# Attention stage of a three-layer kernel: wider matmul streams, other accumulator banks, a shorter step pipeline

## The chip, the cores and the metric

The kernel runs on one core of a Trainium2 chip. The metric is device time in microseconds (us). The kernel before was timed three times: 2105.6, 2106.95 and 2112.1, median 2106.95. A fourth execution was profiled; all rows below come from that one.

The core has a matmul engine (PE, with weight loads shown apart as PEld), a vector engine (DVE), an activation engine (ACT), a general engine (POOL) and a queue that issues transfers (SP). Each takes its instructions in program order. PE writes only to PSUM, which has eight banks of 128 x 512 float32 values.

## The reference

Three layers follow each other: a linear attention with exponential features, a gated layer, and a layer of eight experts. Only the first is touched.

```
q, k, v: (4 batches, 8 heads, 576 tokens, 64); omega: (128, 64)
def phi(x):
    proj = einsum('bhsd,md->bhsm', x, omega)
    h = proj - sum(x*x, axis=-1, keepdims=True)/2
    return exp(h - max(h, axis=-1, keepdims=True)) / sqrt(128)
q_p, k_p = phi(q*scale), phi(k*scale)
kv  = einsum('bhsm,bhsd->bhmd', k_p, v);  z = sum(k_p, axis=2)
num = einsum('bhsm,bhmd->bhsd', q_p, kv)
den = einsum('bhsm,bhm->bhs', q_p, z)[..., None] + 1e-06
x = (num/den) as a matrix (2304 tokens, 512);  out = experts(gated(x))
```

## The kernel before

The attention works through 36 chunks, k and q chunks in turn. A normal chunk holds 512 tokens of two heads (4 blocks of 128 tokens for each head); the remaining 64 tokens of each batch are gathered in two k and two q tail chunks (numbers 0 and 17, 18 and 35). Each chunk passes through a chain of small stages, and the chunks are pipelined by hand: the loop at L639 counts steps, and the table `ORDER` (L63) lists pairs of a stage and an offset. In each step the stages run down the table, stage with offset n on chunk step - n. So the table fixes the order of instructions on every engine.

The stages of one chunk, with the names of tiles in the profile (`two`, `bank` in PSUM; `at` and `turned` in SBUF):

- `s0`, `s0r`, `s0n` (L470, L475, L480): squares on POOL, their sum on DVE, its scaling on ACT.
- `s2p` (L497): projection on PE into one of two double banks `two`; 8 matmuls, two at a time in the two row halves of the array. Offset 1.
- `s2m` (L505): row maximum on DVE; `s2b`, `s2c` (L511, L515): the bias on POOL; `s2x` (L521): 8 exponentials on ACT. Offset 2.
- `s3`: of a k chunk the sums k'v and z, 5 matmuls for each of the two heads (L536, L537), moving 66 columns (64 of v, one of ones, one spare); of a q chunk 8 transposes (L541). Offset 4. The two halves are placed apart in a step: `s30` before the projection, `s31` after it.
- `s3a`: ACT copies what `s3` left in PSUM (L550 for k, L554 for q). Offset 5.
- `s4` (L570; L568 for a tail): numerators and denominators of a q chunk, 4 matmuls of 66 columns for each head; `s4d`, `s4r`, `s4n` (L582, L587, L592) divide on DVE. Offset 6.
- `s5` (L602): 4 transposes of the result; `s5a` (L613) on ACT and `s5b` (L618) on DVE split it in a high and a low part. Offset 7.
- `pump`: twice a step, one piece of background work that converts the weights of the next layer on ACT, DVE and POOL (L192 to L210).
- `warm` (L501): products of an identity matrix with itself, 24 in the first steps, whose results nobody reads.

float32 matmuls show as two records each; the transposes as one. `RINGS` (L67) assigns PSUM banks to uses: turned features `tr3` banks 0 and 3, turned output `tr5` bank 0, k-v sums bank 3, numerators banks 1 and 2. A new use of a bank waits until its last reader is done.

From step 38 on (`step >= NCH + 2`) the gated layer is interleaved with the last steps of the attention; its first matmul is L693. From there on PE has work without a break.

Of the kernel before, what the change touches and what calls it, by code (L numbers as in the profile page):

```python
# [13 lines left out]
AF = mybir.ActivationFunctionType  # L14
ALU = mybir.AluOpType
# [5 lines left out]
P = 128  # L21
B, H, S, D = 4, 8, 576, 64
M = 128
# [18 lines left out]
ZW = D + 2  # L42
# [8 lines left out]
class Kernel:  # L51
    def __init__(self, tc, x, v, vt, omega, wg, wv, wo, w2g, w1, w2, out):
# [7 lines left out]

    ORDER = [("s3a0", 5), ("s3a1", 5), ("s40", 6), ("s41", 6), ("s30", 4), ("s5", 7), ("s2p", 1), ("s31", 4), ("warm", 1),  # L63
             ("s2m", 2), ("s2b", 2), ("s2c", 2), ("s0r", 0), ("s0", -1), ("s5a", 7), ("s5b", 7), ("s2x0", 2), ("s2x1", 2),
             ("s0n", 0), ("s4d0", 6), ("s4d1", 6), ("s4r", 6), ("s4n0", 6), ("s4n1", 6), ("pump", 3), ("pump", 4)]
    WARM = (2, 10, 6, 4, 2)
    RINGS = dict(tr3=(0, 3), tr5=(0,), kv=(3,), nu=(1, 2), a=(0, 1, 2, 3), b=(4, 5, 6, 7))  # L67

    DRAIN = dict(RINGS, tr3=(4, 5), tr5=(6, 4, 5), nu=(7, 6))

# [287 lines left out]
    def run(self):  # L358
        tc, nc = self.tc, self.nc
        with ExitStack() as ctx:  # L360
# [9 lines left out]
            self.twos = [psum.tile([P, 1024], F32, tag=f"b{i}", name=f"two{i}") for i in range(2)]  # L370
            self.turns, self.rings, self.nquad = {}, self.RINGS, 0
            ident = self.cst.tile([P, P], F32, name="ident")
# [23 lines left out]
    def attention(self, m1):  # L396
        tc, nc = self.tc, self.nc
        if True:
# [6 lines left out]
            t5 = af.tile([P, 10, 2, ZW], F32, tag="t5", name="at5")  # L405
# [3 lines left out]
            def turn(name, n):  # L409
                rot[name] = (rot.get(name, -1) + 1) % n  # L410
                return rot[name]
# [6 lines left out]
            vz = [t4[:, i] for i in range(NVZ)]  # L418
# [7 lines left out]
            chunks = [("k", 0, None, None)]  # L426
# [8 lines left out]
            NCH = len(chunks)  # L435
            st = [dict() for _ in chunks]
            kvz = {}
# [3 lines left out]
            def load(i):  # L441
                side, bp, hp, j = chunks[i]
                c = st[i]
                n = 8 if hp is None else 2 * hp + j
                k = turn("x", 3)
                xt = c["xt"] = xts[turn("xt", 4)]
                c["x"] = t0[:, k].rearrange("p (a d) -> p a d", d=D)
                for w, t in ((1, xt), (0, t0[:, k])):
                    nc.sync.dma_start(t, self.x["qk".index(side), w, bp, n])
                c["idx"] = (lambda a, h: 2 * a + h) if hp is None else (lambda a, h: 4 * h + a)  # L450

            def loadv(i):
                side, bp, hp, j = chunks[i]
                c = st[i]
                if side == "q":
                    return
                if hp is None:
                    c["vz"] = vzts[2 * bp:2 * bp + 2]
                    for j in range(2):
                        nc.sync.dma_start(c["vz"][j].rearrange("p a d -> p (a d)"), self.vt[bp, j])  # L460
                else:
                    z = c["vz"] = vz[nvz[0] % NVZ]
                    nvz[0] += 1
                    nc.sync.dma_start(z.rearrange("p a d -> p (a d)"), self.v[bp, 2 * hp + j])

            def s0(i):
                c = st[i]
                x = c["x"]
                xx = c["xx"] = t0[:, 3].rearrange("p (a d) -> p a d", d=D)
                nc.gpsimd.tensor_tensor(xx, x, x, op=ALU.mult)  # L470
# [28 lines left out]
            def warm(i):  # L499
                for _ in range(self.WARM[i] if i < len(self.WARM) else 0):  # L500
                    nc.tensor.matmul(self.banks[1][:, 0:P], ident, ident, start=True, stop=True)  # L501
# [15 lines left out]
            def s2x(i, u):  # L517
                c = st[i]
                e, bi, pr = c["e"], c["bi"], c["pr"]
                for n in range(4 * u, 4 * u + 4):  # L520
                    nc.scalar.activation(e[:, n, :], pr[:, n % 2, n // 2, :], AF.Exp, bias=bi[:, n:n + 1])  # L521

            def s3(i, h):
                side, bp, hp, j = chunks[i]
                c = st[i]
                e = c["e"]
                if side == "k":
                    if hp is None:
                        ek_tail[bp] = (e, c["vz"])
                        return  # L530
                    et, vt = ek_tail[bp]
                    if h == 0:
                        c["kv"] = self.bank("kv", 2, ZW)
                    kv = c["kv"]
                    for a in range(4):
                        nc.tensor.matmul(kv[:, h, :], e[:, c["idx"](a, h), :], c["vz"][:, c["idx"](a, h), :], start=(a == 0), stop=False)  # L536
                    nc.tensor.matmul(kv[:, h, :], et[:, 2 * hp + h, :], vt[j][:, 2 * hp + h, :], start=False, stop=True)  # L537
                else:
                    tr = self.bank("tr3", 4, P)
                    for a in range(4):  # L540
                        nc.tensor.transpose(tr[:, a, :], e[:, c["idx"](a, h), :], ident)  # L541
                    c["tr3", h] = tr

            def s3a(i, h):
                side, bp, hp, j = chunks[i]
                c = st[i]
                if side == "k":
                    if h == 1 and hp is not None:
                        z = t5[:, turn("z", 10)]
                        nc.scalar.activation(z, c["kv"], AF.Copy, scale=1.0 / M)  # L550
                        kvz[bp, hp, j] = z
                else:
                    t = t2[:, turn("et", 4)].rearrange("p (a t) -> p a t", t=P)
                    nc.scalar.copy(t, c["tr3", h])  # L554
                    c["et", h] = t

            def s4(i, h):
                side, bp, hp, j = chunks[i]
                if side == "k":
                    return  # L560
                c = st[i]
                nu = self.bank("nu", 4, ZW)
                for a in range(4):
                    t = c["et", h][:, a, :]
                    if hp is None:
                        for b in range(2):
                            r = slice(b * TL, (b + 1) * TL)
                            nc.tensor.matmul(nu[r, a, :], t[:, r], kvz[bp, a, b][:, h, :], start=True, stop=True)  # L568
                    else:
                        nc.tensor.matmul(nu[:, a, :], t, kvz[bp, hp, j][:, h, :], start=True, stop=True)  # L570
                c["nu", h] = nu

            def s4d(i, h):
                side, bp, hp, j = chunks[i]
# [44 lines left out]
                st[i] = None  # L619

            pump = lambda i: self.attn_pump()
            fns = dict(s0=s0, s0r=s0r, s0n=s0n, s2p=s2p, s2m=s2m, s2b=s2b, s2c=s2c, s4r=s4r, s5=s5, s5a=s5a, s5b=s5b, warm=warm, pump=pump)
            halves = dict(s2x=s2x, s3=s3, s3a=s3a, s4=s4, s4d=s4d, s4n=s4n)

            def stage(n):
                if n in fns:
                    return fns[n]
                g, h = halves[n[:-1]], int(n[-1])
                return lambda i: g(i, h)

            order = [(stage(n), k) for n, k in self.ORDER]
            load(0)
# [3 lines left out]
                nc.tensor.matmul(self.banks[1][:, 0:P], ident, ident, start=True, stop=True)  # L636
            nc.vector.tensor_scalar(om2, om, SCALE, None, op0=ALU.mult)
            s0(0)
            for step in range(NCH + 7):  # L639
                if step == NCH + 2:  # L640
                    self.rings = self.DRAIN
                    self.upper.close()
                    psum = self.upper.enter_context(tc.tile_pool(name="upper", bufs=1, space=PSUM))
                    self.banks += [psum.tile([P, 512], F32, tag=f"b{i}", name=f"bank{i}") for i in range(4, 8)]
                if step + 2 < NCH:
                    load(step + 2)
                if 0 < step <= NCH:
                    loadv(step - 1)
                for fn, n in order:
                    i = step - n  # L650
                    if 0 <= i < NCH:
                        fn(i)
                self.attn_hook(step)
                if step >= NCH + 2:
                    next(m1)

    def attn_hook(self, step):
        if step == 2:
            self.make_tasks()
            self.load_tasks(self.ahead)  # L660
            self.enqueue(6)
# [862 lines left out]
```

## Time and profile before

| what | us |
|---|---|
| median of three runs | 2106.95 |
| the profiled execution | 2111.08 |
| its span in the trace | 2109.3 |
| first matmul of the gated layer (L693) in the trace | 181.51 |
| busy in the span: PE, DVE, ACT, POOL | 2064.3, 1358.7, 810.1, 1003.3 |

The page shows PE busy for 98% of the span, and at 9 tenths or more in nearly all of its 40 slices; the slices below that are in the first 10%. The granted clock of PE is 0.7 in the first slice of the page and 0.9 or more in the others; a slice is 53 us long, so shorter stretches need a closer view. A record of a matmul lasts longer than the distance to the next one, because successive matmuls overlap: what a stream of them costs is read from the starts of successive rows.

### The profile page before, as it was taken

To read this page: it belongs to the slowest core of one execution; us is meant where nothing else is said; L and a number is where in the kernel's file an instruction comes from. 1 tells how busy PE (TensorE), PEld (TensorE's weight loads), DVE (VectorE), ACT (ScalarE), POOL (GpSimd) and SP (SyncE) were. 2 spreads that over 40 slices of the span, in tenths; PEclk is the share of its full clock that TensorE was granted. 3 is DMA by queue.
4 is the path that set the end of the run, shared out by engine and by line. 5 is a ranking of instruction groups with operands and counts; after the bars stand their busy time and mean duration, and the time that the engine had idled before them with its cause. 6 is when DMAs were issued, how large, how long until landed. Compare 5 with 4: busy or idle time off the path is not lost.

```text
span 2109.3 us, 32863 instructions
## 1 busy us (share of the span) xinstructions
PE 2064.3 (98%) x12044; PEld 1992.7 (94%) x12044; DVE 1358.7 (64%) x2175; ACT 810.1 (38%) x1840; POOL 1003.3 (48%) x1014
## 2 busy tenths in 40 slices
PE   8989999999999999999999999999999999999998
PEld 7878999999998889989888999999999999999998
DVE  4764778788755744444445666666688666666666
ACT  5765433333344444334333423233233433323322
POOL 3442657656533455455552544434454544443443
PEclk7999999999999999999999999999999999999999
DMA  5552555555424666666768788877887878877784
GB/s 197 172 161 67 184 167 182 186 165 178 150 86 155 219 219 242 256 224 256 261 226 307 247 262 260 261 260 247 303 262 259 281 259 262 261 259 255 249 273 153
DMA packets 238129, 467.78 MB, mean 222 GB/s; under 512 B 20272, under 2 KB 110096, under 8 KB 233872
## 3 DMA queue, kind: packets, MB, share of 16 engines
q1 hardware_dynamic: 237968, 465.68, 65.6%
q8 instruction: 95, 1.56, 0.3%
q14 instruction: 66, 0.54, 0.1%
HBM read 340.25 MB, written 125.35 MB: 221 GB/s over the span
## 4 chain that ended last, share of the span: by engine, by line
PE 91%; DVE 4%; ACT 2%; issue 1%; POOL 1%; DMA 0%; SPq 0%; DVEq 0%; POOLq 0%; ACTq 0%
PE bank L1049 13%; PE bank L1295 7%; PE bank L1296 7%; PE bank L1297 7%; PE pair L1386 7%; PE pair L1387 7%; PE pair L1388 7%; PE bank L694 5%; PE bank L695 5%; PE bank L693 5%; PE bank L990 4%; PE bank L992 4%; PE bank L991 3%; PE bank L725 2%; PE bank L727 2%; PE bank L726 2%
## 5 line engine op out<-in xcount | busy, mean ns | idle before, releaser
L1398 DVE TENSOR_TENSOR sums<-pair,sums 128x768 f32<-128x768 f32 x209 | 198.8, 951 | 44.3 <-PE pair L1388 44.3
L1295 PE MATMUL bank<-xh,ar 128*128 128x384 f32 x564 | 188.7, 335 | 2.4 <-ACT mt L1328 2.0
L1296 PE MATMUL bank<-xl,ar 128*128 128x384 f32 x564 | 188.4, 334 | 0.0
L1297 PE MATMUL bank<-xh,ar 128*128 128x384 f32 x564 | 188.4, 334 | 0.0
L1065 DVE SCALAR_TENSOR_TENSOR ac<-bank,mt,ac 128x512 f32<-128x512 f32 x84 | 63.1, 751 | 132.5 <-PE bank L1049 128.8
L1386 PE MATMUL pair<-xh,ar 128*128 128x384 f32 x344 | 115.0, 334 | 0.2 <-DVE sums L1398 0.2
L1387 PE MATMUL pair<-xl,ar 128*128 128x384 f32 x344 | 114.9, 334 | 0.0
L1388 PE MATMUL pair<-xh,ar 128*128 128x384 f32 x344 | 114.9, 334 | 0.0
L1295 PEld LDWEIGHTS bank<-xh,ar 128*128 128x128 f32 x564 | 105.8, 188 | 3.4 <-ACT mt L1328 2.7
L1296 PEld LDWEIGHTS bank<-xl,ar 128*128 128x128 f32 x564 | 105.9, 188 | 0.0
L1297 PEld LDWEIGHTS bank<-xh,ar 128*128 128x128 f32 x564 | 105.9, 188 | 0.0
L707 ACT CAST ar<-mt 128x384 fp32r<-128x384 f32 x72 | 37.0, 514 | 170.6 <-DVE mt L704 170.6
L693 PE MATMUL bank<-xh,ar 128*128 128x384 f32 x288 | 96.6, 336 | 0.0
L695 PE MATMUL bank<-xh,ar 128*128 128x384 f32 x288 | 96.2, 334 | 0.0
L695 PE MATMUL bank<-xh,ar1b 128*128 128x384 f32 x288 | 96.2, 334 | 0.0
L694 PE MATMUL bank<-xl,ar 128*128 128x384 f32 x288 | 96.2, 334 | 0.0
L693 PE MATMUL bank<-xh,ar1b 128*128 128x384 f32 x288 | 96.2, 334 | 0.0
L694 PE MATMUL bank<-xl,ar1b 128*128 128x384 f32 x288 | 96.2, 334 | 0.0
L990 PE MATMUL bank<-xh,ar 128*128 128x384 f32 x264 | 89.5, 339 | 3.3 <-DVE st L1024 2.5
L992 PE MATMUL bank<-xh,ar 128*128 128x384 f32 x264 | 88.8, 336 | 0.6 <-DVE ar L262 0.5
L991 PE MATMUL bank<-xl,ar 128*128 128x384 f32 x264 | 88.3, 335 | 0.0
L1049 PE MATMUL bank<-ar,xh 128*128 128x512 f32 x324 | 85.4, 397 | 0.0
(379 smaller groups left out, 6700.8 us busy)
## 6 DMA issues: line engine op xcount, KB each, us to landing
ar<-w2forms SPq DMA_DIRECT2D x144, 512.0 KB, 4.5
ar<-w1forms SPq DMA_DIRECT2D x141, 512.0 KB, 4.9
ar1b<-w1forms SPq DMA_DIRECT2D x62, 512.0 KB, 4.9
ar1b<-w2forms SPq DMA_DIRECT2D x61, 512.0 KB, 4.5
w2forms<-ar SPq DMA_DIRECT2D x224, 128.0 KB, 4.1
w1forms<-ar SPq DMA_DIRECT2D x22, 1280.0 KB, 7.6
sumsraw<-in_w_dram SPq DMA_DIRECT2D x32, 512.0 KB, 4.3
w2forms<-sumsraw SPq DMA_DIRECT2D x128, 128.0 KB, 2.7
```

Source lines behind the costliest of these rows:

```text
L693: nc.tensor.matmul(t, hi[:, c, fs], self.xh[:, c, cs], start=(c == 0), stop=False)
L694: nc.tensor.matmul(t, hi[:, c, fs], self.xl[:, c, cs], start=False, stop=False)
L695: nc.tensor.matmul(t, lo[:, c, fs], self.xh[:, c, cs], start=False, stop=(c == KC - 1))
L990: nc.tensor.matmul(g, ah[:, c, :], bh[:, c, :], start=(first and c == 0), stop=False, skip_group_check=not first)
L1049: nc.tensor.matmul(y, a, w[:, fi % 2, ds], start=(first and x == 0 and k == 0 and fi == fis[0]), stop=(last and x == 1 and fi == fis[-1]))
L1295: nc.tensor.matmul(g, w[:, 0, d], bh[:, d, :], start=bool(first and d == 0), stop=False, skip_group_check=not first)
L1296: nc.tensor.matmul(g, w[:, 0, d], bl[:, d, :], start=False, stop=False, skip_group_check=not first)
L1297: nc.tensor.matmul(g, w[:, 1, d], bh[:, d, :], start=False, stop=(d == 1), skip_group_check=not first)
L1386: nc.tensor.matmul(y, w[:, k, 0, ds], h, start=(k == 0), stop=False)
L1387: nc.tensor.matmul(y, w[:, k, 0, ds], l, start=False, stop=False)
L1388: nc.tensor.matmul(y, w[:, k, 1, ds], h, start=False, stop=(k == 1))
L1398: v.tensor_tensor(a[n], pair, a[n], op=ALU.add)
```

## The change

A k-v matmul and a numerator matmul now stream 128 columns where they streamed 66: `wide` takes a window of 128 neighbouring columns that holds the 66 wanted ones, at its start for the first head and at its end for the second. What is wanted stands in columns 0 to 65 or 62 to 127 of the result, and only that is read. The k-v sums use bank 2 (with the second head's numerators) instead of bank 3, the turned output bank 1 (with the first head's numerators) instead of bank 0. The copy of the k-v sums goes from ACT to a new stage `s3k` on DVE, in the step of the sums. `s3` has offset 3 instead of 4, and `s3a`, `s4`, `s5` follow at 4, 5, 6; both halves of `s3` now stand before the projection, `s5` before `s3`. v is loaded one step earlier, the background work begins one step later, there are 30 warming products instead of 24, and one step less.

```
-    ORDER = [("s3a0", 5), ("s3a1", 5), ("s40", 6), ("s41", 6), ("s30", 4), ("s5", 7), ("s2p", 1), ("s31", 4), ...
+    ORDER = [("s3a0", 4), ("s3a1", 4), ("s40", 5), ("s41", 5), ("s5", 6), ("s30", 3), ("s31", 3), ("s2p", 1), ...
-    WARM = (2, 10, 6, 4, 2)
-    RINGS = dict(tr3=(0, 3), tr5=(0,), kv=(3,), nu=(1, 2), a=(0, 1, 2, 3), b=(4, 5, 6, 7))
+    WARM = (2, 10, 8, 6, 4)
+    RINGS = dict(tr3=(0, 3), tr5=(1,), kv=(2,), nu=(1, 2), a=(0, 1, 2, 3), b=(4, 5, 6, 7))
+            OFF = (0, P - ZW)
+            def wide(t, n, h):
+                o = n * ZW - OFF[h]
+                return t.rearrange("p a d -> p (a d)")[:, o:o + P]
...
-                        c["kv"] = self.bank("kv", 2, ZW)
-                    kv = c["kv"]
+                        c["kv"] = self.bank("kv", 380)
+                    kv = c["kv"][:, h * P:(h + 1) * P]
...
-                        nc.tensor.matmul(kv[:, h, :], e[:, c["idx"](a, h), :], c["vz"][:, c["idx"](a, h), :], start=(a == 0), stop=False)
+                        nc.tensor.matmul(kv, e[:, n, :], wide(c["vz"], n, h), start=(a == 0), stop=False)
...
-                        nc.scalar.activation(z, c["kv"], AF.Copy, scale=1.0 / M)
...
+            def s3k(i):
+                    kv = st[i]["kv"].rearrange("p (h c) -> p h c", h=2)[:, :, 0:ZW]
+                    nc.vector.tensor_scalar(z, kv, 1.0 / M, None, op0=ALU.mult)
...
-                nu = self.bank("nu", 4, ZW)
+                nu = self.bank("nu", 4, P)
+                own = nu[:, :, OFF[h]:OFF[h] + ZW]
...
-                        nc.tensor.matmul(nu[:, a, :], t, kvz[bp, hp, j][:, h, :], start=True, stop=True)
+                        nc.tensor.matmul(nu[:, a, :], t, wide(kvz[bp, hp, j], h, h), start=True, stop=True)
...
-            for step in range(NCH + 7):
+            for step in range(NCH + 6):
-                if 0 < step <= NCH:
-                    loadv(step - 1)
+                if step < NCH:
+                    loadv(step)
...
-        if step == 2:
+        if step == 3:
             self.make_tasks()
```

Two steps on PE (one that sums a k chunk, one that turns a q chunk) in the kernel before; L602 is `s5`, L497 `s2p`, L536 and L537 the k-v sums, L570 the numerators, L541 the turned features:

```order
L602 MATMUL bank_69<-ident,at_97 128x128 x4
L497 MATMUL two_76<-om_100,turned 128x128 x8
L536 MATMUL bank_72<-at_98,at_95 128x66 x4
L537 MATMUL bank_72<-at_98,at_97 128x66
L570 MATMUL bank_70<-at_99,at_96 128x66 x4
L570 MATMUL bank_71<-at_99,at_96 128x66 x4
L541 MATMUL bank_69<-ident,at_95 128x128 x4
L497 MATMUL two_77<-om_100,turned 128x128 x8
L541 MATMUL bank_72<-ident,at_95 128x128 x4
L536 MATMUL bank_72<-at_98,turned 128x66 x4
L537 MATMUL bank_72<-at_98,at_97 128x66
```

The same in the changed kernel, where L613 is `s5`, L543 and L545 the k-v sums, L581 the numerators and L549 the turned features:

```order
L613 MATMUL bank_70<-ident,at_97 128x128 x4
L543 MATMUL bank_71<-at_98,at_95 128x128 x4
L545 MATMUL bank_71<-at_98,at_97 128x128
L543 MATMUL bank_71<-at_98,at_95 128x128 x4
L545 MATMUL bank_71<-at_98,at_97 128x128
L497 MATMUL two_77<-om_100,turned 128x128 x8
L581 MATMUL bank_70<-at_99,at_96 128x128 x4
L581 MATMUL bank_71<-at_99,at_96 128x128 x4
L549 MATMUL bank_69<-ident,at_95 128x128 x4
L549 MATMUL bank_72<-ident,at_95 128x128 x4
L497 MATMUL two_76<-om_100,turned 128x128 x8
```

The projection now ends each step, the k-v sums no longer follow a transpose into their own bank (bank_72 is the fourth, bank_71 the third), and the number of instructions is the same.

Two steps on DVE before, with `s2m` (L505), `s0r` (L475), the division (L582 to L592), `s5b` (L618) and a piece of background work (L203):

```order
L505 TENSOR_REDUCE mx_510<-two_77 128x8
L475 TENSOR_REDUCE ssq_583<-at_94 128x8
L618 TENSOR_TENSOR xl<-bank_69,xh 128x512
L203 TENSOR_SCALAR m1raw_0_1_188<-cv 128x512
L505 TENSOR_REDUCE mx_564<-two_76 128x8
L475 TENSOR_REDUCE ssq_635<-at_94 128x8
L582 TENSOR_SCALAR den_648<-bank_70 128x4
L582 TENSOR_SCALAR den_648<-bank_71 128x4
L587 RECIPROCAL rec_649<-den_648 128x8
L592 TENSOR_TENSOR at_97<-bank_70,rec_649 128x4x64
L592 TENSOR_TENSOR at_97<-bank_71,rec_649 128x4x64
```

And in the changed kernel, where L629 is `s5b` and L565 is `s3k`:

```order
L505 TENSOR_REDUCE mx_486<-two_76 128x8
L475 TENSOR_REDUCE ssq_556<-at_94 128x8
L629 TENSOR_TENSOR xl<-bank_70,xh 128x512
L565 TENSOR_SCALAR at_99<-bank_71 128x132
L196 TENSOR_SCALAR cv<-cv 128x512
L198 TENSOR_SCALAR cv<-cv 128x512
L505 TENSOR_REDUCE mx_542<-two_77 128x8
L475 TENSOR_REDUCE ssq_608<-at_94 128x8
L593 TENSOR_SCALAR den_621<-bank_70 128x4
L593 TENSOR_SCALAR den_621<-bank_71 128x4
L598 RECIPROCAL rec_622<-den_621 128x8
L603 TENSOR_TENSOR at_97<-bank_70,rec_622 128x4x64
```

One instruction has come in, L565 behind `s5b`; what was queued behind `s5b`, the background work and the next step's maximum, is now queued behind L565.

## Rows read from the trace of the kernel before

**Rows 1.** Windows of the trace: busy time (count) by engine, granted clock, DMA share

```profile
28.00:55.50 27.50, 26.83 (x150) 24.36 (x149) 11.06 (x22) 11.67 (x41) 5.47 (x10) 0.50 0.29 97
57.62:93.15 35.53, 32.12 (x322) 28.85 (x322) 25.19 (x46) 26.35 (x91) 18.25 (x31) 1.00 0.55 178
181.51:2109.30 1927.79, 1904.91 (x10619) 1849.31 (x10617) 1249.53 (x1979) 694.51 (x1441) 930.69 (x883) 1.00 0.67 227
```

**Rows 2.** Timeline of PE, two steps: start, length, line, records, [idle before, releaser]

```profile
66.38 0.60 PE L602 MATMUL bank<-ident,at 128*128 128x128 f32 x4
66.91 1.16 PE L497 MATMUL two<-om,turned 64*128 64x128 f32 x16
68.00 1.11 PE L536 MATMUL bank<-at,at 128*128 128x66 f32 x8
...
69.17 1.95 PE L570 MATMUL bank<-at,at 128*128 128x66 f32 x16
70.96 0.61 PE L541 MATMUL bank<-ident,at 128*128 128x128 f32 x4
71.49 1.16 PE L497 MATMUL two<-om,turned 64*128 64x128 f32 x16
72.59 0.66 PE L541 MATMUL bank<-ident,at 128*128 128x128 f32 x4
73.97 1.11 PE L536 MATMUL bank<-at,turned 128*128 128x66 f32 x8 [0.73 <-ACT at L554]
...
75.14 0.60 PE L602 MATMUL bank<-ident,at 128*128 128x128 f32 x4
```

**Rows 3.** Waits of PE from 0 to 200 us: total us, times, longest

```profile
PE bank L536 <- ACT at L554: 15.2, 15, 2.4
```

**Rows 4.** Timeline of PE in the first 33 us

```profile
8.89 2.50 PE L501 MATMUL bank<-ident 128*128 128x128 f32 x20
13.01 1.16 PE L497 MATMUL two<-om,turned 64*128 64x128 f32 x16 [1.63 <-ACT at L521]
14.10 2.60 PE L501 MATMUL bank<-ident 128*128 128x128 f32 x12
...
32.73 3.62 PE L570 MATMUL bank<-at,at 128*128 128x66 f32 x16
```

**Rows 5.** Timeline of PE, two steps at the low clock, first and last row

```profile
43.13 1.06 PE L602 MATMUL bank<-ident,at 128*128 128x128 f32 x4
...
57.62 0.61 PE L602 MATMUL bank<-ident,at 128*128 128x128 f32 x4
```

**Rows 6.** Windows of 5 us: columns as in Rows 1

```profile
15.00:20.00 5.00, 5.00 (x39) 4.65 (x39) 3.36 (x6) 3.04 (x12) 1.64 (x4) 0.71 0.82 269
110.00:115.00 5.00, 5.00 (x39) 4.44 (x40) 1.97 (x3) 3.24 (x12) 0.00 (x0) 0.66 0.23 80
145.00:150.00 5.00, 3.52 (x27) 3.15 (x28) 2.47 (x4) 2.62 (x7) 2.67 (x4) 0.76 0.35 105
```

**Rows 7.** Groups by line, 57.62 to 93.15 us: count | busy us, mean ns | idle before

```profile
L505 DVE TENSOR_REDUCE mx<-two 128x8 f32<-128x1024 f32 x8 | 9.7, 1218 | 0.7 <-PE two L497 0.7
L475 DVE TENSOR_REDUCE ssq<-at 128x8 f32<-128x512 f32 x8 | 5.4, 676 | 0.0
L592 DVE TENSOR_TENSOR at<-bank,rec 128x256 f32<-128x256 f32 x8 | 3.0, 420 | 0.1
L618 DVE TENSOR_TENSOR xl<-bank,xh 128x512 fp32r<-128x512 f32 x4 | 2.8, 692 | 7.0 <-ACT xh L613 7.0
L582 DVE TENSOR_SCALAR den<-bank 128x4 f32<-128x4 f32 x8 | 1.3, 160 | 2.6 <-PE bank L570 2.6
L554 ACT COPY at<-bank 128x512 f32<-128x512 f32 x8 | 4.8, 626 | 0.4 <-PE bank L541 0.4
L511 POOL TENSOR_TENSOR hm<-mx,nsq 128x8 f32<-128x8 f32 x8 | 1.6, 201 | 14.8 <-DVE mx L505 14.6
```

**Rows 8.** Timeline of ACT, the exponentials of one chunk

```profile
58.74 2.18 ACT L521 ACTIVATE at<-two,bi 128x128 f32<-128x128 f32 x8
```

**Rows 9.** Timeline of PE: waits before two stages, first matmul of the gated layer

```profile
146.53 1.11 PE L536 MATMUL bank<-at,at 128*128 128x66 f32 x8 [1.48 <-ACT at L554]
...
181.51 0.42 PE L693 MATMUL bank<-xh,ar 128*128 128x384 f32 x1
181.77 0.34 PE L694 MATMUL bank<-xl,ar 128*128 128x384 f32 x1
181.95 0.33 PE L695 MATMUL bank<-xh,ar 128*128 128x384 f32 x1
```

More of the change, by code (lines that the diff above doesn't have):

```diff
@@ L58, in __init__ @@
         self.bg = deque()
-    ORDER = [("s3a0", 5), ("s3a1", 5), ("s40", 6), ("s41", 6), ("s30", 4), ("s5", 7), ("s2p", 1), ("s31", 4), ("warm", 1),
-             ("s2m", 2), ("s2b", 2), ("s2c", 2), ("s0r", 0), ("s0", -1), ("s5a", 7), ("s5b", 7), ("s2x0", 2), ("s2x1", 2),
-             ("s0n", 0), ("s4d0", 6), ("s4d1", 6), ("s4r", 6), ("s4n0", 6), ("s4n1", 6), ("pump", 3), ("pump", 4)]
-    WARM = (2, 10, 6, 4, 2)
-    RINGS = dict(tr3=(0, 3), tr5=(0,), kv=(3,), nu=(1, 2), a=(0, 1, 2, 3), b=(4, 5, 6, 7))
+    ORDER = [("s3a0", 4), ("s3a1", 4), ("s40", 5), ("s41", 5), ("s5", 6), ("s30", 3), ("s31", 3), ("s2p", 1), ("warm", 1),
+             ("s2m", 2), ("s2b", 2), ("s2c", 2), ("s0r", 0), ("s0", -1), ("s5a", 6), ("s2x0", 2), ("s2x1", 2), ("s0n", 0),
+             ("s4d0", 5), ("s4d1", 5), ("s4r", 5), ("s4n0", 5), ("s4n1", 5), ("s5b", 6), ("s3k", 3), ("pump", 3), ("pump", 4)]
+    WARM = (2, 10, 8, 6, 4)
+    RINGS = dict(tr3=(0, 3), tr5=(1,), kv=(2,), nu=(1, 2), a=(0, 1, 2, 3), b=(4, 5, 6, 7))
     DRAIN = dict(RINGS, tr3=(4, 5), tr5=(6, 4, 5), nu=(7, 6))
@@ L532, in s3 @@
                     if h == 0:
-                        c["kv"] = self.bank("kv", 2, ZW)
-                    kv = c["kv"]
+                        c["kv"] = self.bank("kv", 380)
+                    kv = c["kv"][:, h * P:(h + 1) * P]
                     for a in range(4):
-                        nc.tensor.matmul(kv[:, h, :], e[:, c["idx"](a, h), :], c["vz"][:, c["idx"](a, h), :], start=(a == 0), stop=False)
-                    nc.tensor.matmul(kv[:, h, :], et[:, 2 * hp + h, :], vt[j][:, 2 * hp + h, :], start=False, stop=True)
+                        n = c["idx"](a, h)
+                        nc.tensor.matmul(kv, e[:, n, :], wide(c["vz"], n, h), start=(a == 0), stop=False)
+                    n = 2 * hp + h
+                    nc.tensor.matmul(kv, et[:, n, :], wide(vt[j], n, h), start=False, stop=True)
                 else:
@@ L546, in s3a @@
                 c = st[i]
-                if side == "k":
-                    if h == 1 and hp is not None:
-                        z = t5[:, turn("z", 10)]
-                        nc.scalar.activation(z, c["kv"], AF.Copy, scale=1.0 / M)
-                        kvz[bp, hp, j] = z
-                else:
+                if side == "q":
                     t = t2[:, turn("et", 4)].rearrange("p (a t) -> p a t", t=P)
@@ L555, in s3a @@
                     c["et", h] = t
+            def s3k(i):
+                side, bp, hp, j = chunks[i]
+                if side == "k" and hp is not None:
+                    z = kvz[bp, hp, j] = t5[:, turn("z", 10)]
+                    kv = st[i]["kv"].rearrange("p (h c) -> p h c", h=2)[:, :, 0:ZW]
+                    nc.vector.tensor_scalar(z, kv, 1.0 / M, None, op0=ALU.mult)
             def s4(i, h):
@@ L567, in s4 @@
                             r = slice(b * TL, (b + 1) * TL)
-                            nc.tensor.matmul(nu[r, a, :], t[:, r], kvz[bp, a, b][:, h, :], start=True, stop=True)
+                            nc.tensor.matmul(own[r, a, :], t[:, r], kvz[bp, a, b][:, h, :], start=True, stop=True)
                     else:
-                        nc.tensor.matmul(nu[:, a, :], t, kvz[bp, hp, j][:, h, :], start=True, stop=True)
-                c["nu", h] = nu
+                        nc.tensor.matmul(nu[:, a, :], t, wide(kvz[bp, hp, j], h, h), start=True, stop=True)
+                c["nu", h] = own
             def s4d(i, h):
@@ L621, in attention @@
             pump = lambda i: self.attn_pump()
-            fns = dict(s0=s0, s0r=s0r, s0n=s0n, s2p=s2p, s2m=s2m, s2b=s2b, s2c=s2c, s4r=s4r, s5=s5, s5a=s5a, s5b=s5b, warm=warm, pump=pump)
+            fns = dict(s0=s0, s0r=s0r, s0n=s0n, s2p=s2p, s2m=s2m, s2b=s2b, s2c=s2c, s4r=s4r, s5=s5, s5a=s5a, s5b=s5b, s3k=s3k, warm=warm, pump=pump)
             halves = dict(s2x=s2x, s3=s3, s3a=s3a, s4=s4, s4d=s4d, s4n=s4n)
```

## The prediction

> **What bounds the kernel now.** I began with the page: PE is busy for 98% of the span, and what is missing lies at the start. Windows of the trace [rows 1] part it: from 181.5 us to the end PE is busy for 98.8% at the full granted clock (1.00, that is 2.4 GHz), so what comes before shifts the rest rigidly, and the change is worth what it takes off those first 181.5 us. There the reader is to see two different losses. From 28 to 55.5 us the clock is at 0.50 (1.2 GHz), though PE is busy for 26.8 of 27.5 us; between 57.6 and 93.2 us it is at 1.00, and PE is busy for 32.1 of 35.5 us: it waits. The timeline of two steps [rows 2] shows where: after the second half of the transposes it stands 0.73 us for ACT's copy at L554, since the k-v sums go to the bank that these transposes have just filled. The list of waits [rows 3] counts 15 of these, 15.2 us in all.
>
> From the same starts I read what each stage takes on PE at the full clock [rows 2]: output transposes 0.53 (66.38 to 66.91), projection 1.09, a half of the sums 1.17 (68.00 to 69.17), the numerators 1.79, a half of the turning 0.53.
>
> **128 columns.** 16 k chunks with 10 sums and 16 q chunks with 8 numerators, two records each: 576 records get 62 columns more. What this costs is read from the identity products, which already stream 128: 20 records in 2.50 us [rows 4], 0.125 each, against 16 records of 66 columns in 1.95 [rows 2], 0.122 each. So between 0 and 576 x 0.003 = 1.7 us; I take 0, since the first distance after a projection is in the longer figure. The other bound is a column's price in a long stream: 384 columns in 0.18 us [rows 9], 0.47 ns each, 62 of them 29 ns, 576 times 16.8 us. It can't be below nothing, as no instruction goes.
> The Trainium skill speaks against the edit here ("TensorE: Matmul & The Clock Gate", Back-to-back issue gap): the distance of single matmuls grows by N/2.4 ns, which would make 62 columns cost an estimated 25.8 ns, 14.9 us in all. The two rows just compared do not show it at 66 and 128 columns. The same page (LDWEIGHTS) gives P/1.2 for a weight load, 107 ns for 128 columns, whatever is streamed after it.
>
> **The clock.** Two steps took 14.49 us at the low level [rows 5] and 8.76 at the full one [rows 2]. The low stretch began after waits and went on for 27 us with 66-column matmuls in every step. In the window at 15 us, where identity products and projections run, the clock dropped as well (0.71) and was back soon [rows 4, 6]; the drops at 110 and 145 us were as short (0.66, 0.76). The streams of the changed kernel are like those of the window at 15 us, so I take the short form (0.66 in a window of 5 us is 3.4 us at the half level, 1.7 us lost). The other end is a stretch like that of before, 27 us, whose price is half of it, 13.6 us.
>
> **A step put together.** A step that sums now holds output transposes, both halves of the sums and the projection: 0.53 + 2.34 + 1.09 = 3.96. A step that turns holds numerators, both halves, projection: 1.79 + 1.06 + 1.09 = 3.94. Two steps 7.90 in place of 8.76, if nothing waits. What could:
> - The sums' bank is now the second of the numerators. Its reader is the division on DVE, in the step before; the output transposes, which now come first in the step, need that division anyway. DVE starts a turning step with the maximum 1.22 and the sum 0.68, then 2 x 0.16, a reciprocal (as L582, 0.16) and 2 x 0.42 [rows 7]: done at 3.2 to 3.3 of 3.94 us. Slack 0.6. In the kernel before, half of the sums stood ahead of these transposes.
> - The numerators' first bank must be free of the output (L618 on DVE, done by about 2.6 in the step before) and the second of the sums' copy. That copy moves to DVE; no row has its form. Bounds: 0.16 (L582, 16 elements at most) and 0.42 (L592, 256 elements); by size I take 0.3. DVE's load per two steps is 25.19 / 4 = 6.3 [rows 1], then 6.6 of 7.9; ACT loses as much. The copy waits for the sums (2.87 into the step, when DVE is through 1.22 + 0.68 + 0.69 = 2.6) and ends near 3.4. Behind it on DVE stand the background work and the next maximum, for which ACT waits; half a microsecond of delay there has cover, as follows.
> - Turning three steps behind the load: maximum 1.22, two small POOL instructions of 0.2 [rows 7] and the exponentials 2.18 [rows 8] end 4.0 us after the step that they are in began; the first half is there at 2.9. The earliest user stands at 3.94 + 0.53. Slack 1.6. If the background work on ACT, DVE and POOL eats it, the wait is back.
> - v one step earlier: transfers take 0.55 of the engines' time in these steps [rows 1], so some 0.62 at the new pace. The background work loses one of its 72 turns. Both at nothing; without that cover a late v would stop the first sums only.
>
> **The sum.** Begin at the projection at 13.01 us, whose wait stays. 16 records of identity products (12 took 2.60 [rows 4]) bring 17.6; sums 2.34, projection 1.09, 12 records 1.5: 22.5; turning 1.06, projection, 8 records 1.0: 25.7; sums, projection: 29.1; a whole turning step: 33.1. That is the start of step 8, which before began with the numerators at 32.73 [rows 4]; but the change needs one step less. Steps 8 to 37 are 30 times 3.95 = 118.5. Step 20 has no sums (-2.34), and so step 21 waits for exponentials (+0.6); step 37 has no projection (-1.09): 115.7, up to 148.8 us. In step 38 output transposes 0.53, a wait for the last exponentials 0.6, turning 1.06: the gated layer begins at 151.0. I add what steps take beyond their form: before, four pairs took 35.53 us [rows 1], 8.88 each against 8.76, so 15 x 0.12 = 1.8, and one short drop of the clock, 1.7. That makes 154.5 against 181.51 [rows 9], 27 us sooner. Turning of the last chunk and one output, 1.06 + 0.53, are then already done, which before came later: 28.6 in all.
> Checked from the other side: waits 15.2 at L536, the low clock 27.5 - 27.5/2 = 13.7 and two short drops 3.4 make 32.3; the waits and drops that I leave in bring that to about 28.
> The profiled execution took 2111.08 us, so 2082.5, and I say 2082. The median of the runs is 4.1 lower. If that is a shorter low stretch, the end is the same; if it is something behind it, the changed kernel would stand at 2078.
>
> **Rivals.**
> - The wait stays under another name: DVE is late by more than 0.6 and PE stands at the output transposes, or at the sums for the exponentials. For it: DVE and ACT are near 85% of the new time of a step. Against: the work that comes first on both is short of the step. 16 pairs at 0.75 more: 12, so 2094.
> - The low clock stays for some 27 us, whatever is streamed. For it: the wait at 13 us that comes before the first drop is still there. Price 13.6: 2096.
> - Columns cost what they cost in a long stream, 16.8: 2099. Only the 384-column rows speak for it. The rule of the skill named above would give 14.9 in its place.
> - Two of these together, 25 to 30: about 2108, no change. That is the case in which the change doesn't do what it says.
> - Slower: with exponentials one step before their use, background work (estimated at 0.7 a piece on DVE, as L618 over the same 512 columns [rows 7], and as much or more on POOL) makes PE wait in every pair for about 1.5, and each such wait is followed by a drop, as the one of 1.48 at 146.5 us was [rows 6, 9]. A pair is then 7.9 + 1.5 + 1.7 = 11.1, 16 x (11.1 - 8.88) = 36 more than before, less 17 of low clock that this case would have anyway shed: 2130. It decides from a delay of 1.6 + 1.5 in the chain of each pair; rows 7 don't come near it.
>
> **How the numbers follow.** Forecast 0.60 (2082, own range 2074 to 2092: from no extra wait and the 4.1 below, up to allowances three times as large); wait under another name 0.15; low clock 0.10; columns 0.04; two together 0.06; slower 0.05. A change counts from 0.3%, 6.3 us, which is about what runs of this kernel can tell. The first four cases lie below 2100.6: faster 0.89, same 0.06, slower 0.05. The range goes from 2074 to 2100 and leaves out the last two cases and a little at the lower end.
>
> **What would show it.** First matmul of the gated layer near 154 us; two steps near 8 us; numerators of 16 records again in about 1.95; no wait of the sums for L557 (the copy of L554 under its new number); a granted clock of 1.00 from about 18 us on but for short drops. Wrong, if DVE's division stands as releaser before L613, if windows of 5 us at 0.50 follow each other, or if the gated layer begins after 170 us. That it begins early and the end doesn't follow would break the rigid shift.

## The result and the profile after

The changed kernel took 2079.04 us (median of 4 runs, 2076.95 to 2080.67) against 2109.52 (median of 4, 2105.6 to 2118.03). The ratio is 0.985 with a 95% interval of 0.9816 to 0.9883: 1.5% faster, where 2082 was predicted. The profiled execution took 2080.67 us, its span is 2078.9.

Windows of the trace after (columns as in [rows 1]) show where the time came from.

```profile
10.00:15.00 5.00, 1.91 (x24) 1.60 (x23) 3.46 (x4) 3.45 (x16) 3.69 (x7) 1.00 1.05 395
15.00:20.00 5.00, 5.00 (x31) 5.00 (x31) 1.82 (x2) 3.87 (x15) 1.54 (x4) 0.66 0.77 286
20.00:80.00 60.00, 60.00 (x611) 55.88 (x611) 48.15 (x94) 44.42 (x155) 30.88 (x53) 1.00 0.57 186
80.00:85.00 5.00, 3.65 (x45) 3.17 (x44) 4.10 (x8) 5.00 (x18) 1.44 (x3) 1.00 0.89 295
151.59:2078.90 1927.31, 1904.32 (x10607) 1849.95 (x10605) 1249.20 (x1977) 693.36 (x1439) 930.90 (x883) 1.00 0.68 227
```

Against [rows 1], PE is now busy for all of 20 to 80 us at the full clock. The part from the gated layer on is as long as before, 1927.31 us against 1927.79: the attention gave the whole gain, and the rest was shifted.

The timeline of two steps answers to [rows 2]. It begins with the output transposes (L613) and ends where the next ones begin.

```profile
65.16 0.65 PE L613 MATMUL bank<-ident,at 128*128 128x128 f32 x4
65.65 1.06 PE L543 MATMUL bank<-at,at 128*128 128x128 f32 x8
66.54 0.39 PE L545 MATMUL bank<-at,at 128*128 128x128 f32 x2
66.77 1.06 PE L543 MATMUL bank<-at,at 128*128 128x128 f32 x8
67.66 0.39 PE L545 MATMUL bank<-at,at 128*128 128x128 f32 x2
67.98 1.16 PE L497 MATMUL two<-om,turned 64*128 64x128 f32 x16
69.07 2.05 PE L581 MATMUL bank<-at,at 128*128 128x128 f32 x16
70.96 1.04 PE L549 MATMUL bank<-ident,at 128*128 128x128 f32 x8
71.92 1.16 PE L497 MATMUL two<-om,turned 64*128 64x128 f32 x16
73.02 0.66 PE L613 MATMUL bank<-ident,at 128*128 128x128 f32 x4
```

From 65.16 to 73.02 are 7.86 us without a wait, where [rows 2] have 8.76. The waits of PE in the first 170 us (answering to [rows 3]):

```profile
PE two L497 <- ACT at L521: 3.1, 1, 3.1
PE bank L647 <- POOL ident masks.py:199: 1.4, 1, 1.4
PE bank L581 <- DVE xl L629: 1.3, 1, 1.3
PE bank L613 <- ACT at L521: 1.3, 1, 1.3
PE two L497 <- DVE om L648: 0.3, 1, 0.3
```

The line with 15 waits of the sums is gone. Where the others stand, and where the gated layer begins (L704), the timeline tells, answering to [rows 4, 9]:

```profile
13.84 1.16 PE L497 MATMUL two<-om,turned 64*128 64x128 f32 x16 [3.09 <-ACT at L521]
...
83.97 2.05 PE L581 MATMUL bank<-at,at 128*128 128x128 f32 x16 [1.34 <-DVE xl L629]
...
150.31 0.66 PE L613 MATMUL bank<-ident,at 128*128 128x128 f32 x4 [1.30 <-ACT at L521]
...
151.59 0.42 PE L704 MATMUL bank<-xh,ar 128*128 128x384 f32 x1
```

The gated layer begins at 151.59 us, 29.9 us sooner than in [rows 9]. Groups of DVE in three pairs of steps (57.30 to 80.88 us) have the durations of [rows 7], and the new copy among them:

```profile
L505 DVE TENSOR_REDUCE mx<-two 128x8 f32<-128x1024 f32 x6 | 7.3, 1223 | 2.9 <-PE two L497 2.9
L629 DVE TENSOR_TENSOR xl<-bank,xh 128x512 fp32r<-128x512 f32 x3 | 2.1, 687 | 0.4 <-ACT xh L624 0.4
L565 DVE TENSOR_SCALAR at<-bank 128x132 f32<-128x132 f32 x3 | 0.9, 296 | 0.7 <-PE bank L545 0.7
```

In these steps DVE waits for PE (L505 for the projection, L565 for the sums), and PE for nobody. The division of the pair shown above ends on DVE at 72.34 us, 0.68 ahead of the output transposes at 73.02:

```profile
71.59 0.75 DVE L603 TENSOR_TENSOR at<-bank,rec 128x256 f32<-128x256 f32 x2
```

### The profile page after: what moved, and what is told of

It reads as the page before. It is cut to its first block, busy times and chain, and to the rows that moved or that the text cites. A ratio compares the mean times of both kernels' runs of the same rounds, so it can differ in the third digit from the quotient of the medians.

```text
span 2078.9 us, 32872 instructions
## 1 busy us (share of the span) xinstructions
PE 2048.5 (99%) x12056; PEld 1984.0 (95%) x12056; DVE 1361.1 (65%) x2191; ACT 805.8 (39%) x1824; POOL 1002.9 (48%) x1014
## 4 chain that ended last, share of the span: by engine, by line
PE 95%; DVE 3%; ACT 1%; issue 0%; POOL 0%; DMA 0%; SPq 0%; DVEq 0%; POOLq 0%; ACTq 0%
PE bank L1060 13%; PE bank L1306 7%; PE bank L1308 7%; PE bank L1307 7%; PE pair L1397 7%; PE pair L1398 7%; PE pair L1399 7%; PE bank L706 5%; PE bank L705 5%; PE bank L704 5%; PE bank L1001 4%; PE bank L1003 4%; PE bank L1002 3%; PE bank L736 2%; PE bank L738 2%; PE bank L737 2%
## 5 line engine op out<-in xcount | busy, mean ns | idle before, releaser
L704 PE MATMUL bank<-xh,ar 128*128 128x384 f32 x288 | 96.6, 335 | 0.0
L704 PE MATMUL bank<-xh,ar1b 128*128 128x384 f32 x288 | 96.2, 334 | 0.0
```

The lines of the kernel that those rows point to most:

```text
L704: nc.tensor.matmul(t, hi[:, c, fs], self.xh[:, c, cs], start=(c == 0), stop=False)
```

## The experiments

Which part did it: the streams, the banks, the order or the offsets? Nine kernels, each timed against the kernel before (medians of 2110 us in each of these comparisons).

| kernel | median us | ratio to before, 95% interval |
|---|---|---|
| the change | 2079.04 | 0.9850 (0.9816 to 0.9883) |
| 128 columns alone | 2101.13 | 0.9965 (0.9947 to 0.9984) |
| the change with 66 columns | 2078.69 | 0.9847 (0.9805 to 0.9888) |
| the change with the old banks | 2095.92 | 0.9927 (0.9906 to 0.9948) |
| the change, projection between the halves | 2081.43 | 0.9868 (0.9832 to 0.9903) |
| the change, one step later | 2076.65 | 0.9844 (0.9822 to 0.9866) |
| the change, more work on DVE | 2081.47 | 0.9866 (0.9846 to 0.9885) |
| the change, start mended | 2079.55 | 0.9857 (0.9837 to 0.9878) |
| start mended, 66 columns | 2079.43 | 0.9858 (0.9834 to 0.9881) |
| the new banks alone | 2084.40 | 0.9879 (0.9835 to 0.9924) |

**128 columns alone.** In the kernel before:

```
...
-                        nc.tensor.matmul(kv[:, h, :], e[:, c["idx"](a, h), :], c["vz"][:, c["idx"](a, h), :], start=(a == 0), stop=False)
+                        nc.tensor.matmul(kv, e[:, n, :], wide(c["vz"], n, h), start=(a == 0), stop=False)
...
-                        nc.tensor.matmul(nu[:, a, :], t, kvz[bp, hp, j][:, h, :], start=True, stop=True)
+                        nc.tensor.matmul(nu[:, a, :], t, wide(kvz[bp, hp, j], h, h), start=True, stop=True)
...
```

> The kernel before with 128 streamed columns alone; order, banks and offsets stay. Theory: the long low stretch of the clock (27 us) came with the 66-column streams and shrinks to short drops, while the 15 waits of the sums for ACT's copy stay: the stretch is worth 13.7 us, so 2093 to 2098 us, first matmul of the gated layer near 167 us, two steps still 8.76. Rival, the clock fell because of the waits and the columns don't matter: a long stretch at 0.50 is still there, 2105 to 2112 us.

2101.13 us, 3 us above the upper end of the forecast. In the trace the long stretch at the low clock is gone (windows, columns as in [rows 1]),

```profile
28.00:55.50 27.50, 24.38 (x240) 21.98 (x241) 17.71 (x34) 19.54 (x68) 13.32 (x23) 1.00 0.53 164
57.62:93.15 35.53, 31.93 (x321) 28.55 (x318) 27.13 (x51) 27.59 (x96) 15.02 (x27) 1.00 0.56 177
```

and the waits are all there:

```profile
PE bank L543 <- ACT at L563: 15.7, 15, 2.4
```

So the streams held the clock in this stretch, though PE now stood idle for 3.1 of the 27.5 us, against 0.7 in [rows 1]. The gated layer begins at 170.77 us, 3.8 later than the theory had it; 1.7 of this is a short drop of the clock (0.66 in the window from 100 to 105 us). That wide streams hold the clock where PE waits is borne out. Whether the clock needs them is what the next kernel tests.

**66 columns in the changed kernel.** The same lines taken back in the change.

> The changed kernel with 66 streamed columns again; order, banks and offsets as changed. Theory: after the first drop at 15 us the clock stays low for a long stretch as in the kernel before, some 27 us or more, 13 to 20 us lost: 2092 to 2099 us. Rival, with the waits gone the clock holds whatever is streamed: 2078 to 2081 us. The distance of two records stays 0.112 us at the full clock in both, so columns cost nothing.

2078.69 us: the theory was wrong, the rival right. With 66 columns and no waits the clock stays at 1.00:

```profile
15.00:20.00 5.00, 5.00 (x52) 4.81 (x51) 2.19 (x5) 3.31 (x13) 1.44 (x3) 1.00 0.74 273
28.00:55.50 27.50, 27.50 (x286) 25.77 (x285) 22.57 (x47) 22.19 (x77) 15.76 (x26) 1.00 0.62 194
```

Two steps, first and last row and the numerators between:

```profile
61.86 0.66 PE L613 MATMUL bank<-ident,at 128*128 128x128 f32 x4
...
65.72 2.00 PE L581 MATMUL bank<-at,at 128*128 128x66 f32 x16
67.56 1.04 PE L549 MATMUL bank<-ident,at 128*128 128x128 f32 x8
...
69.62 0.66 PE L613 MATMUL bank<-ident,at 128*128 128x128 f32 x4
```

7.76 us in place of 7.86; the numerators 1.84 (65.72 to 67.56) in place of 1.89. Wide streams cost 0.05 us where a stage of them begins behind matmuls of another kind, and nothing between: twice in a pair (the first half of the sums behind the output transposes, the numerators behind the projection), 0.10 a pair, 1.6 in 16 pairs. Where the numerators follow the sums, as in the kernel with 128 columns alone, they take 1.79 us from start to start, the same as with 66 columns in [rows 2]:

```profile
31.90 1.95 PE L580 MATMUL bank<-at,at 128*128 128x128 f32 x16
33.69 0.60 PE L549 MATMUL bank<-ident,turned 128*128 128x128 f32 x4
```

Nothing is gained by them once the waits are gone.

**The old banks in the changed kernel.**

```
-    RINGS = dict(tr3=(0, 3), tr5=(1,), kv=(2,), nu=(1, 2), ...
+    RINGS = dict(tr3=(0, 3), tr5=(0,), kv=(3,), nu=(1, 2), ...
```

> The changed kernel with the old banks: output transposes in bank 0, k-v sums in bank 3, which the turned features use too. Theory: the banks took the waits away, so PE waits again for ACT's copies of the turned features at the start of each step that sums, about 0.7 us in each of 16 pairs: 11 us more, about 2090 us, two steps about 8.6. Rival, the new order alone removes the waits: 2078 to 2081 us.

2095.92 us, 17 more than the change. The waits are back, now ahead of the output transposes, which share bank 0 with the first half of the turned features:

```profile
PE bank L613 <- ACT at L557: 16.7, 15, 1.7
```

The mean size was 1.1 us a wait, not 0.7. Five of the 15 are 0.79, near the forecast; five are 1.31 to 1.33, and these have background work on ACT in front of the copies. ACT's timeline shows one of them:

```profile
68.36 0.66 ACT L176 CAST ar<-cv 128x512 fp32r<-128x512 f32 x1
68.87 1.13 ACT L557 COPY at<-bank 128x512 f32<-128x512 f32 x2
```

On PE the output transposes then start at 69.56 after a wait of 1.31.

**The new banks in the kernel before.** The same two numbers the other way round, and nothing else.

> The kernel before with the new banks alone (output transposes in bank 1, k-v sums in bank 2); order, offsets, 66 columns, ACT's copy of the sums as before. Theory: the banks alone take the 15 waits of the sums away, since the copy of the turned features is then wanted by nobody on PE until the next turning; the clock holds as well; what stays is that the second head's numerators now follow ACT's copy of the sums closely, 0 to 0.4 us a pair: 2079 to 2088 us. Rival, without the new order the wait only moves to the numerators (for ACT's copy of the sums) at 0.7 to 1 us a pair: 2092 to 2108 us.

2084.40 us: 25.7 less than the 2110.09 that the kernel before took beside it, from two numbers in a table. Two steps, from numerators to numerators:

```profile
67.00 1.95 PE L570 MATMUL bank<-at,at 128*128 128x66 f32 x16
...
74.76 2.00 PE L570 MATMUL bank<-at,at 128*128 128x66 f32 x16
```

7.76 us, as in the changed kernel with 66 columns. The wait that the rival named exists, but is small:

```profile
PE bank L570 <- ACT at L521: 1.7, 1, 1.7
PE bank L568 <- ACT at L550: 1.4, 1, 1.4
...
PE bank L570 <- DVE xl L618: 1.1, 1, 1.1
PE bank L570 <- ACT at L550: 0.9, 3, 0.3
```

The gated layer begins in this trace even 2.6 us sooner than in that of the change:

```profile
148.97 0.67 PE L693 MATMUL bank<-xh,ar 128*128 128x384 f32 x1
```

The start helped: its third projection stands at 12.97 us and no drop follows, where the change has it at 13.84 with a drop. From there to the end this trace takes 1932.63 us, the change 1927.31; one more short drop of the clock (four against three before the last microseconds, each worth at most 1.7 us) is part of that, the rest is not explained. In the median the new banks alone are 5.4 us behind the change, and the intervals of the two overlap. The changed kernel with 66 columns, whose start is like this one's (12.71 us, no drop), begins the gated layer at 147.44, 1.5 sooner. So before the gated layer the banks alone do nearly all that the change does; what streams, order, offsets and the copy on DVE add to them can't be told for certain. Each of the two bank numbers by itself was not run.

**The projection between the halves, in the changed kernel.** In `ORDER` `("s30", 3), ("s2p", 1), ("s31", 3)`.

> The changed kernel with the projection between the two halves of the sums (and of the turning), as before, and not last in a step. Theory: the place of the projection is worth little, since the copy of the sums on DVE still ends before the second head's numerators want the bank: 2077 to 2082 us. Rival, the projection last is what took the waits away: the numerators wait for the copy of the sums by 0.5 to 1 us a pair, 2087 to 2095 us.

2081.43 us, within what the theory gave, and not to be told from the change by the runs. Small waits of the output transposes for the division are new:

```profile
PE bank L613 <- DVE at L603: 1.6, 5, 0.4
```

**One step later.** In `ORDER` offsets 4, 5, 6, 7 for `s3`, `s3a`, `s4`, `s5` and what goes with them, 4 for `s3k`; 43 steps in place of 42.

> The changed kernel with the sums, the turning and all that follows one step later, as before (offsets 4, 5, 6, 7, one more step); order within a step, banks and streams as changed. Theory: two steps stay 7.86, no new wait, one more step of about 4 us and at the change of the batch pair a hiccup of a microsecond or two: 2082 to 2085 us. Rival, the shorter distance costs waits that the longer one doesn't have: no slower than the changed kernel, 2077 to 2080 us.

2076.65 us: the theory was wrong. The step that is added runs beside the gated layer, on whose matmuls PE is busy anyway; its instructions are the same. The distance of the turning to the load is worth nothing that these runs can tell.

**More work on DVE.** A second, unread sum of squares in each step.

```
                 nc.vector.tensor_reduce(c["ssq"], c["xx"], axis=AX.X, op=ALU.add)
...
+                nc.vector.tensor_reduce(t, c["xx"], axis=AX.X, op=ALU.add)
```

> The changed kernel with the sum of squares on DVE done twice in each step (its second result is read by nobody): 0.6 us more of DVE a step. Theory: the division on DVE has 0.7 us of slack before the output transposes want it; this uses it up, and PE then waits for the division (L604) in the pairs in which background work runs on DVE, about 0.4 us a pair: 2083 to 2088 us. Rival, DVE has enough room: no wait, 2078 to 2081 us.

2081.47 us (2081.05 to 2082.02), 2.4 more than the change, whose runs go up to 2080.67: below the 2083 to 2088 of the theory, and by the intervals alone not to be told from the change. The trace decides it. The wait is the one named, in 4 of the 16 pairs (L615 and L605 are L613 and L603 moved by two lines):

```profile
PE bank L615 <- DVE at L605: 2.6, 4, 0.8
```

So the slack of 0.6 to 0.7 us is real: most pairs take the added 0.68 without a wait. Two of the four waits stand behind 1.4 us of background work on DVE (69.28 to 70.69 us, ahead of the wait that ends at 74.22). The other two are in the two pairs after the change of the batch pair, where the changed kernel itself had only 0.33 and 0.09 us left: its divisions end at 87.59 and 94.93 us, its transposes start at 87.92 and 95.02. Other pairs with background work show no wait.

**The start mended.** v loaded a step later again, 18 identity products ahead of the third projection; the second kernel of the pair has 66 columns too.

> The changed kernel with v loaded one step later again (as in the kernel before) and 18 identity products in place of 10 ahead of the third projection. Theory: loading v early held up the second chunk's x and with it the first exponentials by 0.8 us, and the wait of 3.1 us that follows lets the clock drop for 3.4 us (1.7 lost). With both mended the third projection starts near 13.0 instead of 13.84 us without a wait, there is no drop at 15 us, and the gated layer begins 2.0 to 3.0 us earlier: 2075.5 to 2077.5 us. Rival, the start is hidden by the chain of DVE and ACT behind it: no difference, 2079 us.

> As the kernel with 18 identity products and the late v, and 66 columns in the streams again. Theory: where PE doesn't wait, the wide streams keep no clock up and cost 0.05 us at each change of stage, 0.1 us a pair: another 1.6 us, 2074 to 2076 us, two steps 7.76. Rival, without the wide streams the clock drops again somewhere in the attention: 2077 to 2090 us.

2079.55 and 2079.43 us, both above their forecasts: no difference to the change that can be measured, though the traces show the earlier start. Of the first:

```profile
12.57 1.16 PE L497 MATMUL two<-om,turned 64*128 64x128 f32 x16 [0.17 <-ACT at L521]
...
148.69 0.42 PE L704 MATMUL bank<-xh,ar 128*128 128x384 f32 x1
```

The third projection starts 1.3 us earlier with 0.17 of wait left, and the gated layer 2.9 earlier; with 66 columns it begins at 147.26, but without the mended start it did so at 147.44. The reason that I gave, the early v, falls. What the first exponentials wait for is the square of the second chunk on POOL (L470), and that waits for its x, which lands early or late in either form. With v late (128 columns alone):

```profile
8.39 1.04 POOL L470 TENSOR_TENSOR at<-at 128x512 f32<-128x512 f32 x1 [3.19 <-DMA at<-in_x_dram]
```

With v early (the change with 66 columns):

```profile
6.55 1.04 POOL L470 TENSOR_TENSOR at<-at 128x512 f32<-128x512 f32 x1 [1.35 <-DMA at<-in_x_dram]
```

The other traces have this square at 6.77 to 8.63 us, with v late at 6.77 to 8.39 and with v early at 6.55 to 8.63; and in eight of the eleven traces the third projection starts 5.77 to 5.79 us after it. So the 0.8 us are scatter of the transfers, and so are the 1.3 us of the first kernel above, whose square starts at 6.79 where the change has 8.06. The products only fill the wait. Single runs of these two go from 2073.31 to 2081.75, and most of what they differ by goes with the clock: the run of 2073.31 has a mean granted clock of 0.999, the three others of that kernel (2078.97 to 2080.50) have 0.995 or 0.996. A part of that is not in the attention: in the window that answers to 985 us of the change, the second kernel's clock stays up and PE works on.

```profile
981.00:991.00 10.00, 9.55 (x53) 8.91 (x52) 7.14 (x13) 5.93 (x14) 5.82 (x7) 1.00 0.40 133
```

In the change:

```profile
985.00:995.00 10.00, 7.29 (x34) 6.98 (x33) 5.73 (x7) 3.90 (x9) 5.93 (x7) 0.83 0.40 133
```

Two or three microseconds at the start are smaller than this. No version beats the change by more than runs differ.

## Why the prediction was right

- **What bounds it, and the rigid shift.** Right: 29.9 us sooner at the gated layer, 30.4 in the span. The 1.6 us that were to come on top at the end show as 0.5, under short drops of the clock behind that point that differ from trace to trace. Between two traces that have one such drop each (but for the last microseconds), the old order (128 columns alone, 1926.53 us from the gated layer to the end) and the new one (the second kernel with the start mended, 1924.24) are 2.3 apart.
- **A step put together.** 7.90 predicted, 7.86 measured in every regular pair (the two at the change of the batch pair are shorter). The allowance of 0.12 a pair was not needed: with slack on both other engines these pairs have no scatter. Those 1.8 us are a good part of the 3 us between 154.5 (predicted) and 151.59.
- **The waits.** Right in kind and in place, and the banks are their cause: with them the waits come and go in either order (2084.40 with the new banks alone, 2095.92 with all but them). The exponentials were in time for the turning in every pair, as worked out. The copy on DVE took 0.296 us (0.3 taken); the division ended 0.68 us before its user (72.34 against 73.02), 0.6 predicted.
- **128 columns.** 1.6 us, at the upper end of 0 to 1.7, but that is chance. The 1.7 came from the lengths of two rows; by starts, 16 records of 66 and of 128 columns cost the same 1.79 us (second experiment). The 1.6 are what I had set aside, the first distance after a stage of another kind. The Trainium skill ("TensorE: Matmul & The Clock Gate", Back-to-back issue gap) has a rule on single matmuls that would have made an estimated 14.9 us. Neither trace shows that.
- **The clock.** The reason was only half right. The price of 13.6 us is that of one trace's stretch; the streams alone, at their cost of 1.6, gave 10.7 at the gated layer (170.77 against 181.51) and 9 in the median. I took the streams for what ends the low stretch. They do where PE waits (128 columns alone: no long stretch), but without waits it doesn't come with 66 columns either. The four combinations are: 66 with waits, a long stretch; 128 with waits, 66 without, 128 without, none. The long stretch stands in one trace only, but the mean granted clock of the runs says the same: 0.985 to 0.995 in 17 runs of the kernel before (2120.31 us at 0.985, 2100.46 at 0.995), 0.995 to 0.997 in ten with 128 columns alone, 0.995 to 0.998 in eight with the old banks in the changed kernel (128 and waits) and in four of the change with 66. So what the streams alone are worth differs from run to run of the kernel before. That both act is shown, what in the chip weighs them is not.
- **Single waits.** Three were mis-sized. At the start 3.09 us in place of 1.63, from a later landing of x, which comes in traces of either form of the loads. In step 21, 1.34 in place of 0.6, and not for the exponentials but for `s5b` on DVE; its input comes from ACT, where one piece of background work and the two copies of turned features stand in front. In step 38, 1.30 in place of 0.6, since the output transposes there use a bank that belonged to the projection's double banks and so wait for the last exponentials too. Together 2.3 us (the projection 0.83 later, then 0.74 and 0.70).
- **The allowances.** 3.5 us stood against these waits. The 1.8 for scatter went unused. The 1.7 for a short drop was counted twice: the drop came (0.66 at 15 to 20 us), but the sum had paid for it already, as it priced the 16 identity products behind the third projection by the 12 that took 2.60 us in the drop of the kernel before [rows 4, 6]. They took 3.32 us (14.93 to 18.25); in the changed kernel with 66 columns, where no drop came, the same 16 took 1.89 (13.80 to 15.69). Without both allowances the sum gives 151.0, 0.6 below the measured 151.59; the rest of the 2.3 is made up mainly by the numerators of the tail chunk (1.08 us from 91.83 to 92.91, counted as 1.79) and the pairs at 7.86. Errors of both signs met here: that the time came within 3 us is in part luck.
- **One step less.** I counted it as a help for the start of step 8; one step more costs nothing that these runs can tell (2076.65).

## What to carry to other kernels

Where PE waits in a regular rhythm, ask first which two uses share a PSUM bank, and who reads the older one: here two numbers in a table were worth 25.7 us, where the whole change gave 30.5. A remedy for the clock (wider streams, 9 us when alone) is worth nothing once the waits are gone, so test such remedies again after each mended wait. Slack that is worked out from the rows, stage by stage, was right to 0.1 us in the regular pairs; what went wrong was at the seams: start, change of the batch pair, end. And before an allowance for a loss is added, look whether a row that the sum is built from was taken inside that loss.

## What the runs showed of the hardware

PE can be at the low clock for 27.5 us while it is busy for 26.8 of them [rows 1]; being busy in the profile is not being at speed. A float32 matmul took 0.112 us a record from start to start with 66 and with 128 columns (16 records in 1.79 us), and 0.05 us more with 128 only after a change of stage. At the start, a wait of 2.0 to 2.1 us at the third projection was followed by no drop in three traces, one of 2.3 to 3.1 by a drop in five, and the one of 1.63 in the kernel before by a drop too. And runs of one changed kernel differ by 1 to 8 us, those of the kernel before by up to 20, along with their mean granted clock: from 0.985 to 0.995 in its 17 runs, and 0.010 of 2110 us is 21 us. Short drops come in some traces and not in others, hundreds of microseconds after the edit.
